# A decode block with a cached attention: wo behind the last values in three parts, w2 without zero rows, and the first norm on columns

## The chip, the cores and the metric

The kernel runs on one NeuronCore of a Trainium2 chip. The core has TensorE (PE in the rows; PEld is its loading of weights), VectorE (DVE), ScalarE (ACT), GpSimd (POOL) and SyncE (SP), which here issues the loads, and 16 DMA engines that move them. The metric is the device time of one execution in microseconds; the times given are medians of several runs.

## The reference, cut to what matters

Two tokens (B = 2, one position each, D = 512) go through an attention over a cache (32 heads, 4096 keys each, head size 128) and a dense block with a mish activation (F = 1376). Both are modulated by a vector c.

```python
mod = (_silu(c) @ w_mod).reshape(c.shape[0], 6, 1, -1)
sa, ca, ga, sb, cb, gb = (mod[:, i] for i in range(6))
h = _layernorm(x) * (1 + ca) + sa
q = (h @ wq)                                # (2, 32, 1, 128) by heads
p = softmax(q @ k_cache^T * Dh ** -0.5)     # k_cache, v_cache: (2, 32, 4096, 128) fp32
x = x + ga * ((p @ v_cache) as rows @ wo)   # wo: (4096, 512)
h = _layernorm(x) * (1 + cb) + sb
t = h @ w1 + b1                             # w1: (512, 1376)
x = x + gb * ((t * tanh(softplus(t))) @ w2) # w2: (1376, 512)
```

The keys and values are 268 MB in fp32, and each is used once.

## The kernel before

SBUF holds three "rooms" of 64 KB a partition, and everything large passes through them. A list `plan` fixes the order of the loads, and each entry names the room it fills and what must have been used before (`holds`); `used(...)` marks something as used and issues, on SP's queue, every load at the head of the list that may go. In order: `first` (w_mod's first five parts with b1), wq, the keys of head 0, then for heads 1 to 31 a "pair" of 8192 KB (the keys of head h and the values of an earlier one, `behind(h)`; heads 8 and 16 come alone with 4096 KB), then `load_wo` (wo's rows of 30 heads), `load_two` (values of heads 29 and 30, two transfers), `load_last` (values of head 31 in two transfers, wo's last two heads, w1 in two halves) and `load_tail` (mod5 and w2, four transfers; the first holds mod5 and five chunks of w2).

At the start, c and x come by a small transfer of their own (`cx`). x's first norm works on rows: `centred` and `rstd` on a 128x128 layout, with a matmul for the mean (L210) and one for the variance (L216), and the modulation of ca and sa is applied to rows and turned to columns once (L288).

In the loop over heads VectorE multiplies the keys by the query (`products`, L336) and sums them (`scores`, L340). The softmax is short work on VectorE, TensorE and ScalarE. TensorE multiplies values by the exponentials (`values`, L382). Heads are gathered in groups of four (`heads_out`: `totals`, `group_out`), the last four as two groups of two.

After the loop, `project` multiplies 30 heads by wo as rows into `att` (L422), which is copied to `att_sb` (L455) and turned into columns `xps` (L463); the mean of what is known by then (`near`, L481) is set aside. Then come the values of heads 30 and 31, and wo's last two heads are added to `xps` directly as columns (L491: 16 matmuls). From `xps` follow the second norm, w1 (`first_layer`), the activation (L572 to L580, into `actt`), mod5's modulation (L568), four matmuls that are a filler (`idle(4)`, L569), w2's matmuls (L585, chunk by chunk), two steps on VectorE and the output's transfer. w2 stands in 11 chunks of 128 rows, of which the last has 32 zero rows:

```python
WIDTHS = (384, 384, 352, 256)
CHUNKS = [(g, j) for j in range(3) for g in range(4) if WIDTHS[g] > P * j]
```

The program's order on each engine is the order in which it is written (`manual_schedule`), with waits put in for data.

Of the kernel before, what the change touches and what calls it, by code (L numbers as in the profile page):

```python
# [9 lines left out]
BF16 = mybir.dt.bfloat16  # L10
# [4 lines left out]
P = 128  # L15
# [15 lines left out]
WO_FIRST = H - 2  # L31
# [13 lines left out]
def kernel(ctx: ExitStack, tc: tile.TileContext, src: dict, out: bass.AP):  # L45
# [26 lines left out]
    cx = const.tile([16, P], F32, name="cx")  # L72
    nc.scalar.dma_start(out=cx, in_=src["cx"])

# [10 lines left out]
    b1_early = first[:, G * 5 * D :]  # L85
# [11 lines left out]
    def load_wo(n):  # L97
        late["wo"] = room(n, "wo")
        load(late["wo"], 0, src["wo"][:, : WO_FIRST * D])
        w_t["wo"] = late["wo"].rearrange("p (h n) -> p h n", h=H)  # L100

    def load_two(n):
        t = room(n, "two")
        for i in range(2):
            v_t[H - 3 + i] = heads(load(t, i * KV, src["single"][3 + i]))

    def load_last(n):
        t = room(n, "last")
        whole = src["single"][5]
        for a, z in ((0, 6), (6, 8)):  # L110
            load(t, a * KV // 8, whole[:, a * KV // 8 : z * KV // 8])
        v_t[H - 1] = heads(t[:, :KV])
        lo = KV
        load(late["wo"], WO_FIRST * D, src["wo"][:, WO_FIRST * D :])
        w_t["w1"] = t[:, lo : lo + G * F].rearrange("p (k n) -> p k n", k=G)
        for half in (src["w1"][:, : G * F // 2], src["w1"][:, G * F // 2 :]):
            load(t, lo, half)
            lo += G * F // 2
# [33 lines left out]
    def used(*items):  # L152
# [17 lines left out]
    mean_w = const.tile([P, G, R], F32, name="mean_w")  # L170
    nc.vector.tensor_scalar(
        out=mean_w, in0=fold[:, None, :].to_broadcast([P, G, R]), scalar1=1.0 / D, scalar2=None, op0=ALU.mult
    )
    mean_w = mean_w.rearrange("p g r -> p (g r)")
# [29 lines left out]
    def centred(s):  # L204
        rs = const.tile([P, 8], F32, name="rs")
        xc = const.tile([P, P], F32, name="xc")
        sq = const.tile([P, P], F32, name="sq")
        nc.vector.tensor_reduce(out=rs[:, 0:1], in_=s, axis=AX.X, op=ALU.add)
        mps = small_ps("mean_a")
        nc.tensor.matmul(mps[:, 0:1], lhsT=mean_w, rhs=rs[:, 0:1], start=True, stop=True)  # L210
        nc.vector.tensor_scalar(out=xc, in0=s, scalar1=mps[:, 0:1], scalar2=None, op0=ALU.subtract)
        nc.vector.scalar_tensor_tensor(
            sq, xc, 1.0, xc, op0=ALU.mult, op1=ALU.mult, accum_out=rs[:, 1:2]
        )
        vps = small_ps("var_a")
# [3 lines left out]
    def rstd(var, rs):
        nc.scalar.activation(rs[:, 2:3], var, AF.Ln, bias=eps_t[:, 0:1])  # L220
        nc.vector.tensor_scalar(out=rs[:, 4:5], in0=var, scalar1=EPS, scalar2=None, op0=ALU.add)
        nc.scalar.activation(rs[:, 3:4], rs[:, 2:3], AF.Exp, scale=-0.5)
        nc.vector.scalar_tensor_tensor(
            rs[:, 5:6], rs[:, 3:4], rs[:, 4:5], rs[:, 3:4], op0=ALU.mult, op1=ALU.mult
        )
        nc.vector.tensor_scalar(
            out=rs[:, 5:6], in0=rs[:, 5:6], scalar1=-0.5, scalar2=1.5, op0=ALU.mult, op1=ALU.add
        )
        return rs[:, 3:4], rs[:, 5:6]
# [28 lines left out]
    def idle(n):  # L258
        for _ in range(n):
            nc.tensor.matmul(ov[1], lhsT=busy[:, 0:P], rhs=busy, start=True, stop=True)  # L260


    cps = small_ps("cps")[:, : 2 * G * B]
    nc.tensor.matmul(cps, lhsT=cx, rhs=ident[0:16, 0 : 2 * G * B], start=True, stop=True)
    cps, xtps = (cps[:, G * B * i : G * B * (i + 1)].rearrange("p (g b) -> p g b", b=B) for i in range(2))
    xps0 = small_ps("xps0")[:, :P]
    nc.tensor.matmul(xps0, lhsT=place.rearrange("p g r -> p (g r)"), rhs=cx, start=True, stop=True)
    sg = const.tile([P, G, B], F32, name="sg")
    nc.scalar.activation(sg, cps, AF.Exp, scale=-1.0)
    nc.vector.tensor_scalar(out=sg, in0=sg, scalar1=1.0, scalar2=None, op0=ALU.add)  # L270
    nc.vector.reciprocal(sg, sg)
    nc.vector.tensor_tensor(out=ct[:, :, 0:B], in0=cps, in1=sg, op=ALU.mult)
    nc.vector.tensor_copy(two(ct)[:, :, B - 1], ct[:, :, B - 1])
    xt = small("xt")
    nc.vector.tensor_copy(xt, xtps)
    xq = const.tile([P, P], F32, name="xq")
    nc.vector.tensor_copy(xq, xps0)

    xn = const.tile([P, P], F32, name="xn")
    xc, var, rs = centred(xq)  # L280
    y0, y1 = rstd(var, rs)
# [10 lines left out]
    sb, cb = keep(3, ps[:, 0, :]), keep(4, ps[:, 1, :])
    gat, cbt, scale_t = small("gat"), small("cbt"), small("scale_t")
    nc.vector.tensor_copy(gat, columns(ga, "gaps"))
    nc.vector.tensor_scalar(out=cbt, in0=columns(cb, "cbps"), scalar1=1.0, scalar2=None, op0=ALU.add)
    nc.vector.tensor_copy(h2t[:, :, 2 * B : 3 * B], columns(sb, "sbps"))
    nc.vector.tensor_copy(h2t[:, :, B : 2 * B], cbt)
    nc.vector.tensor_tensor(out=scale_t, in0=gat, in1=cbt, op=ALU.mult)
    b1 = const.tile([P, NJ * G * B], F32, name="b1")
    nc.gpsimd.tensor_copy(b1, b1_early)  # L300
# [73 lines left out]
    groups = [list(range(4 * i, 4 * i + 4)) for i in range(H // 4 - 1)] + [[H - 4, H - 3], [H - 2, H - 1]]  # L374
# [44 lines left out]
    def project(hs):  # L419
        for h in hs:  # L420
# [6 lines left out]
                stop=(h >= H - 2 - G),  # L427
# [33 lines left out]
    nc.tensor.matmul(fps, lhsT=ident, rhs=b1, start=True, stop=False, skip_group_check=True)  # L461
    for g in range(G):
        nc.tensor.matmul(  # L463
            xps[:, g], lhsT=late["att_sb"][:, P * g : P * (g + 1)], rhs=fold[:, 0:B],
            start=(g == 0), stop=False, skip_group_check=True,
        )

    def whole(t, name):
        ps = small_ps(name)[:, : G * B]
        nc.tensor.matmul(ps, lhsT=ones, rhs=t, start=True, stop=True)  # L470
        s = const.tile([P, B], F32, name=name)
        nc.vector.tensor_reduce(
            out=s, in_=over_g(ps.rearrange("p (g b) -> p g b", b=B)), axis=AX.X, op=ALU.add
        )
        return s

    xa, offset = small("xa"), small("offset")
    near = const.tile([P, B], F32, name="near")
    nc.vector.tensor_tensor(out=xa, in0=xps, in1=gat, op=ALU.mult)
    nc.vector.tensor_tensor(out=xa, in0=xa, in1=xt, op=ALU.add)  # L480
    near_sum = whole(xa, "near_sum")  # L481
# [179 lines left out]
```

## Time and profile before

| | |
|---|---|
| Median of 3 runs | 698.85 us (698.8 to 699.05) |
| The profiled execution | 698.93 us |
| its span, first to last instruction | 697.2 us |
| HBM read | 297.23 MB, 426 GB/s over the span |
| DVE busy | 587.6 us (84%) |
| PE busy | 292.9 us (42%) |
| mean granted TensorE clock | 0.66 of full speed |
| code loads (queue q8) | 13 packets, 0.21 MB |

The span is what the trace shows; 1.73 us of the profiled execution lie around it. Times in rows are microseconds from the span's start unless marked ns. "Issue to landing" of a transfer counts from its instruction on SP's queue to the semaphore.

### The profile page before, as it was taken

What the parts mean: (1) busy time and instruction counts of PE and PEld (TensorE: products, weight loads), DVE (VectorE), ACT (ScalarE), POOL (GpSimd) and SP (SyncE); (2) the same over time, 40 slices, a digit from 0 to 9 for tenths busy, and PEclk for the clock granted to TensorE, in tenths of its full rate; (3) what the DMA queues carried; (4) which work ended last, traced back from release to release, by engine and by line L of the source; (5) the groups of instructions that cost most, each with busy time, mean ns of one, the idle gap of its engine ahead of it and who ended that gap; (6) DMA issues with size and microseconds to landing.
All of it is one profiled execution on the core that took longest, in us unless ns stands there. A gap on an engine that the chain in (4) does not pass through costs nothing.

```text
span 697.2 us, 4054 instructions
## 1 busy us (share of the span) xinstructions
PE 292.9 (42%) x1679; PEld 100.6 (14%) x1680; DVE 587.6 (84%) x240; ACT 39.5 (6%) x187; POOL 4.7 (1%) x22
## 2 busy tenths in 40 slices
PE   2360435432350435443504453444322453443886
PEld 1110101110110101111101111111100111110244
DVE  3039999999899999999999999999999899999102
ACT  1000000000000000000000000000000000000000
POOL 2000000000000000000000000000000000000000
PEclk9775565666655666566655558665765566556879
DMA  9999999999999999999999999999999999999996
GB/s 407 406 448 425 432 456 429 422 429 440 445 429 425 426 440 440 432 430 416 446 440 430 432 432 437 432 429 440 429 433 432 426 440 432 433 432 413 434 418 252
DMA packets 6686, 297.49 MB, mean 427 GB/s; under 512 B 756, under 2 KB 780, under 8 KB 1292
## 3 DMA queue, kind: packets, MB, share of 16 engines
q1 hardware_dynamic: 6636, 297.23, 98.8%
q8 instruction: 13, 0.21, 0.1%
q14 instruction: 5, 0.04, 0.0%
q10 hardware_dynamic: 32, 0.01, 0.0%
HBM read 297.23 MB, written 0.00 MB: 426 GB/s over the span
## 4 chain that ended last, share of the span: by engine, by line
DMA 49%; DVE 45%; PE 5%; issue 0%; ACT 0%; SPq 0%; DVEq 0%
DMA kv<-in_pair 40%; DVE kv L336 22%; DVE s L340 21%; DMA two<-in_single 4%; PE ov L382 2%; DMA tail<-in_w 2%; DMA first<-in_mod 2%; PE modps L241 1%; DVE n L358 1%; DVE n L357 1%; PE yps L585 0%; PE otp L398 0%; PE att L422 0%; PE last_ps L463 0%; DVE m L350 0%
## 5 line engine op out<-in xcount | busy, mean ns | idle before, releaser
L336 DVE TENSOR_TENSOR kv<-kv,qb 128x8192 f32<-128x8192 f32 x32 | 277.9, 8684 | 44.2 <-DMA kv<-in_pair 22.5
L340 DVE TENSOR_REDUCE s<-kv 128x64 f32<-128x8192 f32 x32 | 277.4, 8667 | 0.0
L382 PE MATMUL ov<-kv,e 128*32 128x512 f32 x928 | 168.6, 893 | 5.2 <-ACT e L366 5.2
L362 PE MATMUL mb<-n,ones 2*128 2x2 f32 x64 | 17.7, 344 | 221.4 <-DVE n L358 221.4
L321 PE MATMUL qb<-q_sb,row_of 32*128 32x512 f32 x32 | 28.4, 1035 | 65.4 <-DVE kv L336 65.4
L382 PEld LDWEIGHTS ov<-kv,e 128*32 128x32 f32 x928 | 36.9, 156 | 118.7 <-issue 109.6
L362 PEld LDWEIGHTS mb<-n,ones 2*128 2x128 f32 x64 | 15.8, 303 | 230.3 <-issue 155.5
L352 PE MATMUL mt<-ident,m 128*2 128x128 f32 x64 | 13.7, 300 | 75.8 <-DVE m L350 75.8
L363 ACT COPY m<-mb 128x2 f32<-128x2 f32 x32 | 5.1, 160 | 532.2 <-PE mb L362 423.7
L366 ACT ACTIVATE e<-s,m 128x32 f32<-128x32 f32 x64 | 20.0, 314 | 1.2
L321 PEld LDWEIGHTS qb<-q_sb,row_of 32*128 32x128 f32 x32 | 8.8, 302 | 73.7 <-DVE kv L336 67.8
L352 PEld LDWEIGHTS mt<-ident,m 128*2 128x2 f32 x64 | 3.1, 82 | 97.4 <-DVE m L350 76.7
L410 DVE RECIPROCAL total<-l 128x8 f32<-128x8 f32 (+1 forms) x9 | 1.7, 184 | 14.7 <-PE l L408 14.7
L308 PE MATMUL qps<-wq,ht 128*32 128x512 f32 x64 | 9.5, 761 | 10.5 <-DMA wq<-in_wq 10.5
L366 ACT ACTIVATION_READ_ACCUMULATOR e<-s,m 128x1 f32 x64 | 11.9, 186 | 0.0
L398 PE MATMUL otp<-pick,o 128*128 128x8 f32 (+1 forms) x72 | 9.5, 258 | 3.9 <-ACT o L394 3.9
L382 PE MATMUL ov<-two,e 128*32 128x512 f32 x64 | 9.7, 763 | 0.3 <-DMA two<-in_single 0.3
L422 PE MATMUL att<-wo,ot 128*2 128x512 f32 x60 | 9.6, 742 | 0.4 <-DVE ot L401 0.3
L398 PEld LDWEIGHTS otp<-pick,o 128*128 128x128 f32 x72 | 8.7, 191 | 5.5 <-ACT o L394 5.5
L401 DVE TENSOR_TENSOR ot_last<-otp,total 128x4 f32<-128x4 f32 x1 | 0.2, 163 | 11.0 <-PE otp L398 11.0
L357 DVE TENSOR_REDUCE n<-mt 2x1 f32<-2x128 f32 x32 | 8.7, 272 | 0.5 <-PE mt L352 0.5
L394 ACT COPY o<-ov 128x512 f32<-128x512 f32 x9 | 5.3, 586 | 61.4 <-PE ov L382 61.4
(140 smaller groups left out, 107.2 us busy)
## 6 DMA issues: line engine op xcount, KB each, us to landing
kv<-in_single SPq DMA_DIRECT2D x3, 4096.0 KB, 31.1
two<-in_single SPq DMA_DIRECT2D x2, 4096.0 KB, 34.3
wo<-in_wo SPq DMA_DIRECT2D x1, 7680.0 KB, 39.1
first<-in_mod SPq DMA_DIRECT2D x1, 5132.0 KB, 15.1
last<-in_single SPq DMA_DIRECT2D x1, 3072.0 KB, 27.6
last<-in_w SPq DMA_DIRECT2D x2, 1376.0 KB, 34.7
tail<-in_w SPq DMA_DIRECT2D x1, 2304.0 KB, 16.2
last<-in_single SPq DMA_DIRECT2D x1, 1024.0 KB
```

The source lines that it names most:

```text
L241: nc.tensor.matmul(ps[R * g : R * (g + 1)], lhsT=ct[:, k, :], rhs=t[:, k, :].rearrange("p (m n) -> p m n", m=n)[:, :, P * g : P * (g + 1)] ...
L308: nc.tensor.matmul(ps[R * g : R * (g + 1)], lhsT=ht[:, k, :], rhs=w_t["wq"][:, k, 512 * c : 512 * (c + 1)], start=(k == 0), stop=(k == G - 1),
L321: nc.tensor.matmul(qb[:, b], lhsT=row_of[R * g : R * (g + 1), b], rhs=q_sb[R * g : R * (g + 1), half], start=True, stop=True,)
L336: nc.vector.tensor_tensor(out=k_t[h], in0=k_t[h], in1=qv, op=ALU.mult)
L340: nc.vector.tensor_reduce(out=s_t[h].rearrange("p b j -> p (b j)"), in_=k_t[h].rearrange("p b j d -> p (b j) d"), axis=AX.X, op=ALU.add,)
L352: nc.tensor.matmul(mps[h], lhsT=m_t[h][:, 0:2], rhs=ident, start=True, stop=True)
L357: nc.vector.tensor_reduce(out=n[:, 0:1], in_=mps[h], axis=AX.X, op=ALU.max, negate=True)
L362: nc.tensor.matmul(bps[:, 0:2], lhsT=ones[0:B, :], rhs=n[:, 1:3], start=True, stop=True)
L366: nc.scalar.activation(e_t[h % 4][b][:, :, lo : lo + 4], s_t[h][:, b].rearrange("p (c m) -> p c m", m=4), AF.Exp, bias=m[:, 2 + b : 3 + b] ...
L382: nc.tensor.matmul(ov[i % 2][R * g : R * (g + 1), :], lhsT=e_t[h % 4][b][:, c, :], rhs=v_t[h][:, b, 4 * c : 4 * c + 4, :].rearrange("p m d ...
L398: nc.tensor.matmul(tps[:, :n], lhsT=o[:, m, :], rhs=pick[:, m, at : at + n], start=(m == 0), stop=(m == 3))
L422: nc.tensor.matmul(att[R * g : R * g + B, :], lhsT=ot[:, B * h : B * (h + 1)], rhs=w_t["wo"][:, h, :], start=(h < G), stop=(h >= H - 2 - G),)
```

## The change

The first load carries c and x as columns beside b1, the transfer `cx` goes, and the first norm is computed on columns by functions that the second norm uses as well (`whole`, `centred`, `root`, `times_root`); ca and sa are turned to columns each. The mean `near` and `offset` are taken from x alone, at the start. The order of the late loads becomes: values of heads 29 and 30 in one transfer, values of head 31, all of wo in three parts (16, 12 and 4 heads), w1 in two halves, mod5 alone, w2 in five parts. All 32 heads are projected as rows after the last values; the direct addition of the last two heads as columns goes, and so do the two groups of two heads and the filler. w2's 12 chunks have 128 rows but for the last two, which have 64 and 32; these two come from sources of shape (8, 8, 512) and (4, 8, 512), cut from arrays with a ninth row of zeros that is not read, and their matmuls use only as many rows.

```diff
-WIDTHS = (384, 384, 352, 256)
+WIDTHS = (384, 384, 320, 288)
...
+SIZES = [min(P, WIDTHS[g] - P * j) for g, j in CHUNKS]
...
-WO_FIRST = H - 2
+WO_PARTS = (0, 16, 28, 32)
+PARTS = ((0, 6), (10, 11), (11, 12), (6, 9), (9, 10))
...
-    cx = const.tile([16, P], F32, name="cx")
-    nc.scalar.dma_start(out=cx, in_=src["cx"])
...
     def load_two(n):
-        t = room(n, "two")
-        for i in range(2):
-            v_t[H - 3 + i] = heads(load(t, i * KV, src["single"][3 + i]))
+        piece = load(room(n, "two"), 0, src["two"])
+        v_t[H - 3], v_t[H - 2] = heads(piece[:, :KV]), heads(piece[:, KV:])
...
+    def load_wo(n):
+        t = room(n, "wo")
+        w_t["wo"] = t.rearrange("p (h n) -> p h n", h=H)
+        for a, z in zip(WO_PARTS, WO_PARTS[1:]):
+            load(t, a * D, src["wo"][:, a * D : z * D])
+        for i in range(2):
+            load(late["w1"], i * G * F // 2, src["w1"][:, i * G * F // 2 : (i + 1) * G * F // 2])
...
     def load_tail(n):
         t = room(n, "tail")
...
+        w_t["mod5"] = load(t, 0, src["mod5"]).rearrange("p (k n) -> p k n", k=G)
+        w2 = t[:, G * D : (G + NCH) * D]
+        w_t["w2"] = w2.rearrange("p (c n) -> p c n", c=NCH)
+        for i, (a, z) in enumerate(PARTS):
+            nc.sync.dma_start(out=w2[: SIZES[a], a * D : z * D], in_=src["w2"][i])
...
-        (load_wo, None),
         (load_two, [("v", H - 3), ("v", H - 2)]),
         (load_last, None),
+        (load_wo, None),
...
+    def root(v_sum, name):
+        st = const.tile([P, 4, B], F32, name=f"st_{name}")
+        nc.scalar.activation(st[:, 0], v_sum, AF.Ln, bias=eps_t[:, 0:1], scale=1.0 / D)
+        nc.scalar.activation(st[:, 1], st[:, 0], AF.Exp, scale=-0.5)
...
+    early = const.tile([P, (NJ + 2) * G * B], F32, name="early")
+    nc.gpsimd.tensor_copy(early, early_in)
...
     ps = modulation("0", 0, 3, w_t["mod"])
...
+    mod = [keep("012", ps)]
     ps = modulation("3", 3, 2, w_t["mod"])
...
+    mod.append(keep("34", ps))
+
+    near = const.tile([P, B], F32, name="near")
+    near_sum = whole(xt, "x_sum_a")
+    h, sq = centred(xt, near_sum, "a")
...
+    times_root(root(whole(sq, "v_sum_a"), "a"), h)
+    nc.vector.scalar_tensor_tensor(h, columns(mod[0][:, 1], "caps"), 1.0, h, op0=ALU.add, op1=ALU.mult)
+    nc.vector.tensor_tensor(out=ht[:, :, 0:B], in0=columns(mod[0][:, 0], "saps"), in1=h, op=ALU.add)
...
-    groups = [list(range(4 * i, 4 * i + 4)) for i in range(H // 4 - 1)] + [[H - 4, H - 3], [H - 2, H - 1]]
+    groups = [list(range(4 * i, 4 * i + 4)) for i in range(H // 4)]
...
-    project(range(H - 4))
-    values(H - 3)
...
-    project((H - 4, H - 3))
...
+    for h in range(H - 3, H):
+        values(h)
+        heads_out(h)
...
+    project(range(H))
+    nc.scalar.copy(late["att_sb"], att)
     for g in range(G):
...
-    values(H - 2)
-    values(H - 1)
-    group_out(len(groups) - 1, ot_last)
-    for i in range(2):
-        for g in range(G):
-            nc.tensor.matmul(
-                xps[:, g],
-                lhsT=w_t["wo"][:, H - 2 + i, P * g : P * (g + 1)],
...
-    idle(4)
...
-    for n in range(NCH):
+    chunks = [n for a, z in PARTS for n in range(a, z)]
+    for n in chunks:
         for t in range(G):
             nc.tensor.matmul(
                 yps[R * t : R * (t + 1), :P],
-                lhsT=actt[:, n, :],
-                rhs=w_t["w2"][:, n, P * t : P * (t + 1)],
...
+                lhsT=actt[: SIZES[n], n, :],
+                rhs=w_t["w2"][: SIZES[n], n, P * t : P * (t + 1)],
...
+    def part(a, z):
+        size = SIZES[a]
+        if size == P:
+            return join(w2[:, a:z])
+        t = np.zeros((size // 8, 9, D), w2.dtype)
+        t[:, :8] = w2[:size, a].reshape(size // 8, 8, D)
+        return t
```

## Rows read from the trace of the kernel before

**Rows 1.** The page: DMA share in 40 slices (tenths), and VectorE's two costliest groups.
```profile
DMA  9999999999999999999999999999999999999996
...
L336 DVE TENSOR_TENSOR kv<-kv,qb 128x8192 f32<-128x8192 f32 x32 | 277.9, 8684 | 44.2 <-DMA kv<-in_pair 22.5
L340 DVE TENSOR_REDUCE s<-kv 128x64 f32<-128x8192 f32 x32 | 277.4, 8667 | 0.0
```

**Rows 2.** SP's queue in order of time, from 606 us: start, us, instruction, count.
```profile
606.88 0.33 SPq L69 DMA_DIRECT2D wo<-in_wo  x1
626.24 0.80 SPq L69 DMA_DIRECT2D two<-in_single  x2
645.59 0.80 SPq L69 DMA_DIRECT2D last<-in_single  x2
...
646.91 0.91 SPq L69 DMA_DIRECT2D last<-in_w  x2
672.92 1.75 SPq L69 DMA_DIRECT2D tail<-in_w  x4
```

**Rows 3.** The tail load's issues (first and last), and its last part's time to landing.
```profile
L69 SPq DMA_DIRECT2D tail<-in_w x4: 327/422/430, 672.9 to 674.2; - x4
...
tail<-in_w SPq DMA_DIRECT2D x1, 256.0 KB, 18.6
```

**Rows 4.** The chain that ended last, from 672 us: start, us, what.
```profile
672.92 16.16 DMA tail<-in_w
...
689.22 1.08 PE modps L241 x32
...
690.46 0.81 PE ov L260 x3
691.27 2.58 PE yps L585 x88
```

**Rows 5.** Windows of 1 us at the stream's end: busy time by engine, PEclk, DMA share, GB/s.
```profile
689.00:690.00 1.00, 0.78 (x29) 0.81 (x32) 0.64 (x4) 0.00 (x0) 0.00 (x0) 1.00 0.69 274
690.00:691.00 1.00, 0.84 (x15) 0.34 (x7) 0.00 (x0) 0.27 (x1) 0.00 (x0) 1.00 0.40 158
691.00:692.00 1.00, 1.00 (x32) 0.80 (x33) 0.00 (x0) 0.00 (x0) 0.00 (x0) 1.00 0.29 107
692.00:693.00 1.00, 1.00 (x48) 1.00 (x43) 0.00 (x0) 0.00 (x0) 0.00 (x0) 1.00 0.02 8
```

**Rows 6.** Windows of 4 us around the projection; the first busy time is TensorE's.
```profile
647.00:651.00 4.00, 3.80 (x22) 1.01 (x26) 0.37 (x1) 0.88 (x5) 0.00 (x0) 0.61 0.97 418
651.00:655.00 4.00, 4.00 (x40) 0.85 (x32) 0.00 (x0) 0.00 (x0) 0.00 (x0) 0.97 1.04 444
661.00:665.00 4.00, 3.75 (x15) 2.06 (x15) 0.34 (x2) 0.59 (x1) 0.00 (x0) 0.56 0.96 412
```

**Rows 7.** The timeline from 661 to 690 us: start, us, engine, line, instruction.
```profile
661.36 1.76 PE L422 MATMUL att<-wo,ot 128*2 128x512 f32 x4 [0.25 <-DVE ot L401]
...
663.20 0.59 ACT L455 COPY last<-att 128x512 f32<-128x512 f32 x1 [3.20 <-DMA two<-in_single]
...
678.88 1.95 PE L491 MATMUL last_ps<-ot_last,wo 128*128 128x2 f32 x16 [0.25 <-DVE ot_last L401]
680.86 0.17 DVE L502 TENSOR_TENSOR u<-last_ps,scale_t 128x8 f32<-128x8 f32 x1 [2.04 <-PE last_ps L491]
...
689.58 0.20 DVE L580 TENSOR_TENSOR last<-f 128x22 f32<-128x22 f32 x1
```

**Rows 8.** The timeline of the start, to 36 us.
```profile
7.49 0.18 ACT L269 ACTIVATE sg<-cps 128x8 f32<-128x8 f32 x1 [5.04 <-PE cps L264]
...
8.44 0.17 DVE L273 COPY ct<-ct 128x4 f32<-128x4 f32 x1
...
23.72 0.33 SPq L69 DMA_DIRECT2D kv<-in_pair  x1
...
35.30 1.08 PE L308 MATMUL qps<-wq,ht 128*32 128x512 f32 x4 [10.53 <-DMA wq<-in_wq]
```

More of the change, by code (lines that the diff above doesn't have):

```diff
@@ L95, in load_keys @@
         k_t[h], v_t[behind(h)] = heads(piece[:, :KV]), heads(piece[:, KV:])
[L97 to L100, printed above, removed]
     def load_two(n):
-        t = room(n, "two")
-        for i in range(2):
-            v_t[H - 3 + i] = heads(load(t, i * KV, src["single"][3 + i]))
+        piece = load(room(n, "two"), 0, src["two"])
+        v_t[H - 3], v_t[H - 2] = heads(piece[:, :KV]), heads(piece[:, KV:])
     def load_last(n):
         t = room(n, "last")
[L109 to L118, printed above, removed]
+        v_t[H - 1] = heads(load(t, 0, src["single"][3]))
+        late["w1"] = t[:, KV : KV + G * F]
+        w_t["w1"] = late["w1"].rearrange("p (k n) -> p k n", k=G)
+        lo = KV + G * F
         for name, n_cols in (("att_sb", 512), ("hq_pad", NJ * P), ("actt", NCH * R)):
@@ L219, in rstd, with whole @@
[L219 to L224, printed above, removed]
-        )
[L226 to L229, printed above, removed]
+    def whole(t, name):
+        ps = small_ps(name)[:, : G * B]
+        nc.tensor.matmul(ps, lhsT=ones, rhs=t, start=True, stop=True)
+        s = const.tile([P, B], F32, name=name)
+        nc.vector.tensor_reduce(
+            out=s, in_=over_g(ps.rearrange("p (g b) -> p g b", b=B)), axis=AX.X, op=ALU.add
+        )
+        return s
@@ new lines, in centred @@
+    def centred(x, x_sum, name):
+        xm, sq = small(f"xm_{name}"), small(f"sq_{name}")
+        nc.vector.scalar_tensor_tensor(xm, each_g(x_sum), -1.0 / D, x, op0=ALU.mult, op1=ALU.add)
+        nc.vector.tensor_tensor(out=sq, in0=xm, in1=xm, op=ALU.mult)
+        return xm, sq
+    def root(v_sum, name):
+        st = const.tile([P, 4, B], F32, name=f"st_{name}")
+        nc.scalar.activation(st[:, 0], v_sum, AF.Ln, bias=eps_t[:, 0:1], scale=1.0 / D)
+        nc.scalar.activation(st[:, 1], st[:, 0], AF.Exp, scale=-0.5)
+        nc.vector.tensor_scalar(
+            out=st[:, 2], in0=v_sum, scalar1=-0.5 / D, scalar2=-0.5 * EPS, op0=ALU.mult, op1=ALU.add
+        )
+        return st
@@ L231, in columns, with times_root @@
+    def times_root(st, t):
+        for _ in range(2):
+            nc.vector.tensor_tensor(out=st[:, 2], in0=st[:, 2], in1=st[:, 1], op=ALU.mult)
+        nc.vector.tensor_tensor(out=t, in0=t, in1=each_g(st[:, 1]), op=ALU.mult)
+        nc.vector.scalar_tensor_tensor(t, each_g(st[:, 2]), 1.5, t, op0=ALU.add, op1=ALU.mult)
     def columns(s, name):
@@ L256, in small @@
         return const.tile([P, G, B], F32, name=name)
[L258 to L267, printed above, removed]
@@ L268 @@
-    sg = const.tile([P, G, B], F32, name="sg")
-    nc.scalar.activation(sg, cps, AF.Exp, scale=-1.0)
+    early = const.tile([P, (NJ + 2) * G * B], F32, name="early")
+    nc.gpsimd.tensor_copy(early, early_in)
+    c_in, xt = (early[:, G * B * i : G * B * (i + 1)].rearrange("p (g b) -> p g b", b=B) for i in range(2))
+    b1 = early[:, 2 * G * B :]
+    sg = small("sg")
+    nc.scalar.activation(sg, c_in, AF.Exp, scale=-1.0)
     nc.vector.tensor_scalar(out=sg, in0=sg, scalar1=1.0, scalar2=None, op0=ALU.add)
@@ L271 @@
     nc.vector.reciprocal(sg, sg)
-    nc.vector.tensor_tensor(out=ct[:, :, 0:B], in0=cps, in1=sg, op=ALU.mult)
+    nc.vector.tensor_tensor(out=ct[:, :, 0:B], in0=c_in, in1=sg, op=ALU.mult)
     nc.vector.tensor_copy(two(ct)[:, :, B - 1], ct[:, :, B - 1])
[L274 to L281, printed above, removed]
@@ L292 @@
[L292 to L296, printed above, removed]
+    ps = modulation("0", 0, 3, w_t["mod"])
+    mod = [keep("012", ps)]
+    ps = modulation("3", 3, 2, w_t["mod"])
+    mod.append(keep("34", ps))
@@ new lines @@
+    near = const.tile([P, B], F32, name="near")
+    near_sum = whole(xt, "x_sum_a")
+    h, sq = centred(xt, near_sum, "a")
+    nc.vector.tensor_scalar(out=near, in0=near_sum, scalar1=1.0 / D, scalar2=None, op0=ALU.mult)
+    times_root(root(whole(sq, "v_sum_a"), "a"), h)
+    nc.vector.scalar_tensor_tensor(h, columns(mod[0][:, 1], "caps"), 1.0, h, op0=ALU.add, op1=ALU.mult)
+    nc.vector.tensor_tensor(out=ht[:, :, 0:B], in0=columns(mod[0][:, 0], "saps"), in1=h, op=ALU.add)
+    gat, cbt, scale_t, offset = (small(n) for n in ("gat", "cbt", "scale_t", "offset"))
@@ L297 @@
+    nc.vector.tensor_copy(gat, columns(mod[0][:, 2], "gaps"))
+    nc.vector.tensor_scalar(
+        out=cbt, in0=columns(mod[1][:, 1], "cbps"), scalar1=1.0, scalar2=None, op0=ALU.add
+    )
+    nc.vector.tensor_copy(h2t[:, :, 2 * B : 3 * B], columns(mod[1][:, 0], "sbps"))
     nc.vector.tensor_copy(h2t[:, :, B : 2 * B], cbt)
     nc.vector.tensor_tensor(out=scale_t, in0=gat, in1=cbt, op=ALU.mult)
-    b1 = const.tile([P, NJ * G * B], F32, name="b1")
-    nc.gpsimd.tensor_copy(b1, b1_early)
+    nc.vector.tensor_tensor(out=offset, in0=xt, in1=each_g(near), op=ALU.subtract)
@@ L302 @@
+    nc.vector.tensor_tensor(out=offset, in0=offset, in1=cbt, op=ALU.mult)
     q_sb = const.tile([P, 2, 4 * DH], F32, name="q_sb")
@@ L464 @@
             xps[:, g], lhsT=late["att_sb"][:, P * g : P * (g + 1)], rhs=fold[:, 0:B],
[L465 removed]
+            start=(g == 0), stop=(g == G - 1), skip_group_check=True,
         )
[L468 to L481, printed above, removed]
[L482 to L501 removed]
+    u, x2, xg = small("u"), two(x2t), small("xg")
     nc.vector.tensor_tensor(out=u, in0=xps, in1=scale_t, op=ALU.mult)
     nc.vector.tensor_tensor(out=h2t[:, :, 0:B], in0=u, in1=offset, op=ALU.add)
[L504 to L510 removed]
+    nc.vector.tensor_tensor(out=xg, in0=xps, in1=gat, op=ALU.mult)
+    nc.vector.tensor_tensor(out=x2, in0=xg, in1=xt, op=ALU.add)
+    x_sum = whole(x2, "x_sum_b")
+    _, sq = centred(x2, x_sum, "b")
     w1ps = wide_ps("w1ps")
@@ L526 @@
     first_layer(0)
-    v_sum = whole(sq2, "v_sum")
+    v_sum = whole(sq, "v_sum_b")
     for k in range(1, G):
         first_layer(k)
-    st = const.tile([P, 6, B], F32, name="st")
-    nc.scalar.activation(st[:, 0], v_sum, AF.Ln, bias=eps_t[:, 0:1], scale=1.0 / D)
-    nc.scalar.activation(st[:, 1], st[:, 0], AF.Exp, scale=-0.5)
-    nc.vector.tensor_scalar(
-        out=st[:, 2], in0=v_sum, scalar1=-0.5 / D, scalar2=-0.5 * EPS, op0=ALU.mult, op1=ALU.add
-    )
+    st = root(v_sum, "b")
     nc.vector.scalar_tensor_tensor(st[:, 3], x_sum, 1.0 / D, near, op0=ALU.mult, op1=ALU.subtract)
@@ L586 @@
                 yps[R * t : R * (t + 1), :P],
[L587 to L590 removed]
+                lhsT=actt[: SIZES[n], n, :],
+                rhs=w_t["w2"][: SIZES[n], n, P * t : P * (t + 1)],
+                start=(n == chunks[0]),
+                stop=(n == chunks[-1]),
             )
@@ L634, in _lay_out @@
         "wo": join(rows(a["A_wo"])),
-        "w2_0": join(wm[:, :, 5 * D :], w2[:, :5]),
         "w1": join(rows(a["B_w1"])),
-        "w2_1": join(w2[:, 5:8]),
-        "w2_2": join(w2[:, 8:10]),
-        "w2_3": join(w2[:, 10:]),
+        "two": join(head_rows(v, H - 3), head_rows(v, H - 2)),
+        "mod5": join(wm[:, :, 5 * D :]),
+        **{f"w2_{i}": part(*p) for i, p in enumerate(PARTS)},
     }
@@ L654 @@
         ).ap()
-    src["w2"] = [src.pop(f"w2_{i}") for i in range(4)]
+    src["w2"] = [src.pop(f"w2_{i}") for i in range(len(PARTS))]
+    src["w2"] = [t[:, :8] if len(t.shape) == 3 else t for t in src["w2"]]
     out = nc.dram_tensor("out", inputs["A_x"].shape, F32, kind="ExternalOutput").ap()
```

81 lines of the change are left out of this document (8 added, 73 removed).

## Prediction

> **What bounds the kernel now.** I read the page's slices first. The DMA engines are at nine tenths or more in 39 of 40 slices, while VectorE spends 8.68 + 8.67 = 17.35 us on a head [rows 1]. Then SP's queue: it issues 8192 KB on a room's release every 19.35 us (606.88, 626.24, 645.59), so a load takes longer than VectorE's two passes, and two loads are always in flight [rows 2]. Hence the stream of bytes sets the time, at 8192 / 19.35 = 423 KB/us; a chunk of w2 (128 rows, 256 KB over sixteen engines) is worth 0.605 us. Only two things can move the end: how many bytes the busiest DMA engine carries, and what follows the last landing.
>
> Next the landings. The last part of w2 is issued at 674.2 and lands 18.6 later, at 692.8 [rows 3]. The chain shows that the end does not hang on it: it goes through the first part of the tail load (mod5 and five chunks in one transfer, landed at 689.09), then modps 1.08, the filler of `idle` 0.81, and the matmuls of w2, 2.58, up to 693.85 [rows 4]. From there to the span's end at 697.2 are 3.35 us, which both kernels pay. So about one microsecond lies between the last landing and the end of w2's matmuls, and most of it is modps and filler waiting behind a large first part.
>
> Last, how the stream ends. The DMA share falls to 0.69, 0.40 and 0.29 in the three microseconds from 689, and to 0.02 from 692 [rows 5]. A quarter of the engines, some four of sixteen, still work more than a microsecond after the rest are done. If all ended together, it would be near 689 + 0.69 + 0.40 + 0.29 + 0.02 = 690.4, two microseconds earlier. No view says which engines these are.
>
> **Part by part.** *First norm on columns.* c and x now ride at the end of the first load, so SiLU starts at its landing, not before it: from the exponential to ct took 7.49 to 8.61, 1.1 us, plus the small copy on POOL [rows 8]. Modulation starts about 1.5 us later and releases its room at some 25.2 instead of 23.72. The norm's two sums now stand behind both modulations on TensorE, so ht comes near 29. Both are covered: SP has 8192 KB of wq and 4096 KB of keys queued in front, and wq's matmuls wait for their load until 35.30 after 10.53 us of idleness [rows 8]. Cost nothing; without that cover 1.5 us. The cx transfer (8 KB) goes and its bytes come back in the first load: nothing.
>
> *Order of the loads.* The bytes are the same, and SP's rooms are released by the same scores as before (606.88, 626.24, 645.59), so the stream has no new hole. The tail load waits for the values of heads 29 and 30. Their room now lands near 648, so it is issued before 662 instead of 672.92, while the queue holds work until 684. SP issues 5 transfers after 645.59 in place of 5, and 6 in place of 4 in the tail, 0.43 each, all into a full queue: nothing.
>
> *w2's parts.* Before, every engine carried eleven chunks. The last 96 rows now come from sources whose leading sizes are 8 and 4. I take it that they go to eight and to four engines: then eight engines carry ten chunks, four carry eleven and four twelve. If the late engines are among the eight, the last landing moves from 692.8 to 692.2. Spread evenly (10.75 chunks) it is 692.65; if the late ones carry twelve it is 693.4. I take 692.2: eight of sixteen engines win, four lose, and the end is set by engines that were late already. The Trainium skill ("DMA: Bandwidth & Descriptors", Rules for kernel authors) says to use all 16 engines, since a leading dimension below 16 confines a transfer to that many; by it the four doubly loaded engines would end the stream at 693.4. The ends in [rows 5] are uneven, which that rule does not weigh, and they do not say which engines are late. The same page (Why a DMA increments its semaphore by 16 and not by 1) has the count as the largest number up to 16 that divides both leading sizes, and the engines as the lowest numbered; no row here shows it.
>
> *Landings counted back from 692.2* at 423 KB/us, on an engine with ten chunks: last chunk 692.2; three before it 691.6; the first six 689.8; mod5 (1024 KB) 686.15; w1's halves 683.7 and 680.5; wo's parts (4096, 3072, 1024 KB) 667.5, 674.8 and 677.2; the last values 657.9.
>
> *The projection.* All heads now go as rows, behind the landings. Values of head 31 (32 matmuls, at 3.8 us for 22 in the slower stretch) and the group's output are done before 667.5. Such a matmul took 4.00/40 = 0.10 us at clock 0.97 and 3.80/22 = 0.17 at 0.61 [rows 6]. The first 16 heads (32 matmuls) take 3.2 to 5.5 us and are done by 673. The next 12 (24) start at 674.8 and take 2.4 to 4.1; the last 4 (8) start at 677.2 and take 0.8 and 0.5 of drain. I take the faster pace, since TensorE has worked from 667.5 on: 678.6. Copy to att_sb 0.59 plus 0.1 [rows 7]: 679.3. Eight column matmuls are half of sixteen that took 1.95 [rows 7]: 680.3. Before, u started at 680.86 [rows 7]. So the chain that follows is some 0.5 us early.
>
> *From u to the activation.* Nothing in it changes but a few columns in a copy. It took 680.86 to 689.78 [rows 7], 8.92: now 680.3 to 689.2. mod5 has long landed, so modps (1.08) runs right behind the hidden layer's matmuls, from some 687.6, under the vector work; filler 0.81 is gone.
>
> *w2's matmuls.* They wait for the first six chunks: 689.8 and 0.05. Twelve chunks at 2.58/11 each are 2.81: 692.7. The last chunk landing at 692.2 allows 692.2 + 0.05 + 0.23 and a drain of 0.25, 692.75. So 692.75 against 693.85: **1.1 us less**. The profiled execution took 698.93 with 1.73 us around its span, and the median is 0.08 below it: 698.85 - 1.1 = 697.75, which I round up to **697.9** for the 64 and 128 KB transfers and their unseen price.
>
> *Removed and costed at nothing:* the row form's small constants and copies on VectorE before 16 us, one group output and the near_sum step in the tail; they lay beside loads or in the chain already replaced. Bounds: nothing to 0.3 us gained.
>
> **What the clock may do.** The stretches in [rows 6] show both levels, 0.5 and 1.0 of full speed (1.2 and 2.4 GHz), as means: 0.61 while TensorE came out of light work, 0.97 once it had run dense matmuls. At 661 to 665 it was back at 0.56, after some two microseconds of small matmuls [rows 6], and the two heads projected there took 1.76 [rows 7]. The Trainium skill ("TensorE: Matmul & The Clock Gate", HAM oscillation) says that waits for loads between bursts gate TensorE to 1.2 GHz each time. By that rule the new projection, which waits for three landings, would run at half clock: the second rival. The row at 651 is against it for dense work, the one at 661 for it behind a lull.
>
> **Rivals.** (1) *The late engines are not among the eight.* For: [rows 5] don't name them, and half of all engines lie elsewhere. Against: only four of sixteen lose. Spread evenly or on engines that keep eleven chunks: first six chunks 0.45 to 0.6 later, end at 693.2 to 693.3, 698.3. On the four with twelve: 693.4 + 0.53 = 693.9, 698.9.
>
> (2) *TensorE falls to half clock in the projection's waits; this is the slower side.* Place: between the first and second part of wo it idles one to three microseconds. Price: 32 matmuls at twice 0.10 from 674.8 are 6.4, then 0.5 of drain, copy 0.7, columns 1.9: 684.3 instead of 680.3; activation 693.2, w2's matmuls 696.0, against 693.85: 2.15 more, 701.0. If the clock comes back half way, 2 us of it are lost: about 699.0. It decides from the point where u starts later than 682.1 (even), and by 0.2% later than 683.5. Against: the burst before the wait is dense and the wait short. Without the filler the same fall could strike w2's matmuls themselves: 5.6 from 689.85 is 695.5, 700.5.
>
> (3) *The lateness goes away.* If the four engines are late by chance of this arrangement (code loads, order of transfers), the stream ends by 691.5 and only the activation at 689.2 binds: 692.1, 697.1.
>
> (4) *Nothing happens*, as the end hangs on the stream: gains of landing and tail cancel against later chunks. That is rival 1 in numbers, 698.3 to 698.9.
>
> **How the numbers follow.** Forecast 0.50, 697.9, own range 697.1 to 698.6. Rival 1 with 4: 0.22 (698.3 to 698.9). Rival 2: 0.16, of which 0.10 beyond 700.2. Rival 3: 0.12, 697.1. What a measurement here can tell from no change is about 0.2%, 1.4 us: below 697.45 is faster, above 700.25 slower. Faster: 0.12 and a fifth of the forecast's half, 0.22. Slower: 0.10. Same: 0.68. The range 697.1 to 699.4 leaves out the deep end of rival 3 and the slow part of rival 2.
>
> **What would show it.** Right: chain through the last parts of the tail load, with modps ahead of the activation; the tail load issued before 662; w2's matmuls starting near 689.9 and ending near 692.8 with waits for chunks; projection's last matmuls near 678.5 at clock 1.0. Wrong: u after 682, or a DMA share that keeps a quarter after 692; w2's matmuls well over 0.03 us apiece; modulation or wq's matmuls late enough that a load's issue moves from 606.88.

## The result and the profile after

The kernel after took 700.85 us (median of 20 runs, 699.58 to 702.07), the one before 699.0 (20 runs, 698.48 to 700.55): ratio 1.0022, 95% interval 1.0015 to 1.0029 (ratios here are taken over all runs; the two medians alone give 1.0026). That is slower, by a little over the 0.2% named in the prediction; forecast were 697.9 and a range of 697.1 to 699.4. The profiled execution of after took 701.02 us, with a span of 699.2.

The chain that ended last in after, from 656 us (start, us, what), which answers to [rows 4]:

```profile
656.27 0.33 SPq L70
656.60 0.44 issue
657.04 33.72 DMA tail<-in_w
690.76 0.14 issue
690.90 5.09 PE yps L514 x96
695.99 0.03 issue
```

Two numbers hold the loss. The first part of w2, its first six chunks, lands at 690.76 (657.04 + 33.72) where the forecast had 689.8. And the 96 matmuls of w2 take 5.09 us where it had 2.81. They end at 695.99, against 693.85 before.

Windows of 1 us of after (start:end, us, busy time of PE, PEld, DVE, ACT and POOL, PEclk, DMA share, GB/s), to be held against [rows 5]:

```profile
686.00:687.00 1.00, 0.82 (x10) 0.80 (x14) 0.00 (x0) 0.48 (x4) 0.00 (x0) 1.00 1.01 281
687.00:688.00 1.00, 1.00 (x33) 0.75 (x32) 0.59 (x4) 0.23 (x1) 0.00 (x0) 1.00 0.99 289
688.00:689.00 1.00, 0.02 (x4) 0.00 (x0) 0.55 (x3) 0.27 (x1) 0.00 (x0) 1.00 0.94 231
689.00:690.00 1.00, 0.00 (x0) 0.00 (x0) 0.00 (x0) 0.00 (x0) 0.00 (x0) 1.00 1.00 297
690.00:691.00 1.00, 0.10 (x4) 0.13 (x8) 0.00 (x0) 0.00 (x0) 0.00 (x0) 1.00 0.80 279
691.00:692.00 1.00, 1.00 (x37) 1.00 (x40) 0.00 (x0) 0.00 (x0) 0.00 (x0) 0.88 0.47 190
692.00:693.00 1.00, 1.00 (x23) 0.62 (x19) 0.00 (x0) 0.00 (x0) 0.00 (x0) 0.50 0.28 100
```

The same view of before, for the microsecond ahead of [rows 5]:

```profile
688.00:689.00 1.00, 0.15 (x2) 0.06 (x1) 0.49 (x3) 0.22 (x1) 0.00 (x0) 1.00 0.95 381
```

Read the last two columns together. From 686 to 690 the DMA engines of after are busy (0.94 to 1.01), and yet move only 231 to 297 GB/s; from 685 to 686 it was 406, and before had 381 from 688 to 689 at a share of 0.95. So the engines do not wait for work: each transfer takes longer. The packets in the trace (the pieces that a transfer is cut into, with the time of each) say the same: those of the first six chunks, 12288 bytes each, took 460 to 472 ns from 684 to 685 and 615 to 791 ns from 686 to 690, without exception. Then read PEclk: TensorE does nothing from 688.0 to 690.9, keeps its full clock to nearly 692, and then runs at 0.50 (1.2 GHz), in the middle of w2's matmuls.

The timeline of after (start, us, engine, line, instruction, idle time before it), beside [rows 7]:

```profile
667.00 5.71 PE L399 MATMUL att<-wo,ot 128*2 128x512 f32 x32 [4.09 <-DMA wo<-in_wo]
...
674.22 3.62 PE L399 MATMUL att<-wo,ot 128*2 128x512 f32 x32 [1.50 <-DMA wo<-in_wo]
...
679.63 0.17 DVE L444 TENSOR_TENSOR u<-last_ps,scale_t 128x8 f32<-128x8 f32 x1 [16.75 <-PE last_ps L436]
...
686.94 1.08 PE L227 MATMUL modps<-tail,ct 128*32 128x128 f32 x32
...
688.45 0.20 DVE L508 TENSOR_TENSOR last<-f 128x24 f32<-128x24 f32 x1
690.87 1.60 PEld L514 LDWEIGHTS yps<-tail,last 128*32 128x32 f32 x48 [3.11 <-issue]
690.90 5.05 PE L514 MATMUL yps<-tail,last 128*32 128x128 f32 x96 [2.88 <-DMA tail<-in_w]
```

Up to the activation the forecast holds. wo's parts land at 666.9 and 674.2 (forecast 667.5 and 674.8); the projection is done at 677.84 (forecast 678.1 without its drain), u starts at 679.63 (680.3), modps at 686.94 (687.6), and the activation ends at 688.65 (689.2). All is 0.3 to 0.7 us early, and then TensorE waits 2.88 us for a landing.

### The profile page after: what moved, and what is told of

Same layout as the page of the kernel before. It is cut to its first block, busy times and chain, and to the rows that moved or that the text cites. A ratio compares the mean times of both kernels' runs of the same rounds, so it can differ in the third digit from the quotient of the medians.

```text
span 699.2 us, 3990 instructions
## 1 busy us (share of the span) xinstructions
PE 281.3 (40%) x1658; PEld 94.4 (14%) x1658; DVE 582.5 (83%) x230; ACT 39.4 (6%) x185; POOL 4.5 (1%) x21
## 4 chain that ended last, share of the span: by engine, by line
DMA 52%; DVE 42%; PE 4%; issue 0%; SPq 0%; POOL 0%; ACT 0%; DVEq 0%
DMA kv<-in_pair 45%; DVE kv L313 21%; DVE s L317 20%; DMA tail<-in_w 5%; DMA first<-in_mod 2%; PE ov L359 2%; PE modps L227 1%; PE yps L514 1%; DVE n L335 1%; PE qb L298 1%; DVE n L334 0%; DVE m L327 0%; PE mb L339 0%; SPq L70 0%; PE mt L329 0%
## 5 line engine op out<-in xcount | busy, mean ns | idle before, releaser
L359 PE MATMUL ov<-kv,e 128*32 128x512 f32 x928 | 162.7, 866 | 5.0 <-ACT e L343 5.0
L227 PE MATMUL modps<-first,ct 128*32 128x384 f32 (+1 forms) x64 | 7.0, 609 | 17.7 <-DVE ct L254 17.7
L387 DVE RECIPROCAL total<-l 128x8 f32<-128x8 f32 x8 | 1.5, 187 | 13.6 <-PE l L385 13.6
L375 PE MATMUL otp<-pick,o 128*128 128x8 f32 x64 | 8.5, 259 | 3.2 <-ACT o L371 3.2
```

The lines of the kernel that those rows point to most:

```text
L227: nc.tensor.matmul(ps[R * g : R * (g + 1)], lhsT=ct[:, k, :], rhs=t[:, k, :].rearrange("p (m n) -> p m n", m=n)[:, :, P * g : P * (g + 1)] ...
L359: nc.tensor.matmul(ov[i % 2][R * g : R * (g + 1), :], lhsT=e_t[h % 4][b][:, c, :], rhs=v_t[h][:, b, 4 * c : 4 * c + 4, :].rearrange("p m d ...
L375: nc.tensor.matmul(tps[:, :n], lhsT=o[:, m, :], rhs=pick[:, m, at : at + n], start=(m == 0), stop=(m == 3))
```

## Experiments

Two causes were to be told apart: the clock (a filler gone, a wait of 2.88 us) and the landings (something in the new parts of w2 slows every transfer). A third question was whether the forecast's choice of engines was right.

**1. after with a filler** behind mod5's modulation: twelve matmuls on a tile of zeros, `idle` as in before.

```diff
...
     gps = modulation("5", 0, 1, w_t["mod5"])
+    idle(12)
```

> The changed kernel with twelve filler matmuls between mod5's modulation and w2's matmuls, so that TensorE is busy until the first six chunks of w2 land. Theory A (two costs: the stream's last microseconds are slowed, and TensorE, idle for 2.9 us before w2's matmuls, falls to half clock in them): the 96 matmuls run at 0.03 us apiece, about 2.8 us in place of 5.1, first six chunks still land near 690.8; end of w2's matmuls near 693.8, time near 699.0, ratio to before 0.999 to 1.001. Theory B (the late landings alone cost the time): the end moves by less than 0.5 us, ratio 1.0015 to 1.003. Theory C (the filler is all that was lost): the ratio falls below 0.9985, since the shorter path pays out.

Measured: 699.68 us (11 runs), 1.0012 [1.0003, 1.0021], span 697.5. From its chain, then its window at 692:

```profile
657.04 33.84 DMA tail<-in_w
690.88 0.14 issue
691.01 3.27 PE yps L521 x96
```

```profile
692.00:693.00 1.00, 1.00 (x36) 0.57 (x27) 0.00 (x0) 0.00 (x0) 0.00 (x0) 1.00 0.31 107
```

The landing is as late as in after (690.88), the clock stays at 1.00, and the 96 matmuls take 3.27 us instead of 5.09. So the clock is a cause, worth 1.82 us in these profiles and 0.0010 of the ratio (some 0.7 us; the two intervals overlap, after's runs lie 2.5 us apart, and its profiled execution is above their median). What remains, 1.0012, is not of the clock; it is a little more than I had thought would remain.

**2. after with plain w2:** eleven chunks of 128 rows again, the zero rows back; the rest of the change stays.

```diff
-WIDTHS = (384, 384, 320, 288)
+WIDTHS = (384, 384, 352, 256)
-SIZES = [min(P, WIDTHS[g] - P * j) for g, j in CHUNKS]
+SIZES = [P] * NCH
-PARTS = ((0, 6), (10, 11), (11, 12), (6, 9), (9, 10))
+PARTS = ((0, 6), (6, 9), (9, 10), (10, 11))
```

> The changed kernel with w2 as before: eleven chunks of 128 rows, the last with 32 zero rows, in four parts, every part over all rows. Theory A: the DMA engines keep above 380 GB/s until 689, the first six chunks land near 690.0 and the last near 692.8; TensorE still idles some 2 us before w2's matmuls, so the clock can still fall in some executions: ratio 0.9990 to 1.0015, with a spread of over 1 us. Theory B: the ratio is 0.999 or less in all executions. Theory C: as the changed kernel, 1.0015 to 1.003.

Measured: 698.36 us, 0.9991 [0.9982, 1.0], span 696.5. Its windows:

```profile
686.00:687.00 1.00, 0.94 (x14) 0.93 (x18) 0.07 (x1) 0.38 (x4) 0.00 (x0) 1.00 1.01 424
687.00:688.00 1.00, 0.90 (x32) 0.63 (x24) 0.64 (x5) 0.26 (x2) 0.00 (x0) 1.00 1.00 410
688.00:689.00 1.00, 0.00 (x0) 0.00 (x0) 0.42 (x3) 0.23 (x1) 0.00 (x0) 1.00 0.91 363
```

With 64 KB more to move, the stretch that ran at 231 to 289 GB/s runs at 363 to 424, and w2's matmuls start before 690. The 96 thin rows are worth 0.0031 of the ratio (1.0022 less 0.9991), the filler's 0.0010 among them: without the late landing the wait is 1.69 us, and in this execution the clock stays up by itself. The edit also drops the twelfth chunk and changes the order of the parts; number 7 keeps both as in after. The rest of the change gains 0.0009, some 0.6 us, with an interval that touches 1.

**3. after with plain w2 and a filler:** the edit of 2 with `idle(8)`.

> The changed kernel with w2 as before (128-row chunks) and eight filler matmuls, 1.7 us, between mod5's modulation and w2's matmuls. Theory A: the stream ends as with plain w2 (0.9991), the clock can no longer fall in the wait: ratio 0.9980 to 0.9992, and a narrower spread. If the last landing alone sets the end: the same ratio as with plain w2, to 0.0003.

Measured: 698.36 us, 0.9986 [0.9978, 0.9995]: the one version here whose interval lies wholly below 1. From 2 it can't be told.

**4. after, thin parts over sixteen engines:** the sources are (64, 512) and (32, 512), without the ninth row.

```diff
-        t = np.zeros((size // 8, 9, D), w2.dtype)
-        t[:, :8] = w2[:size, a].reshape(size // 8, 8, D)
-        return t
+        return np.ascontiguousarray(w2[:size, a])
```

> The changed kernel with the parts of 64 and 32 rows from sources without the ninth row, shapes (64, 512) and (32, 512), so that they can spread over all sixteen engines. If confinement to eight and four engines slows the stream (theory A): the stretch of 231 to 297 GB/s from 687 to 690 is gone, as with plain w2, and the first six chunks land before 690.2. If thin parts as such slow it: the stretch stays under 300 GB/s and the landing is 690.5 or later. The clock's share of the cost is the same in both: ratio 1.000 to 1.002.

Measured: 701.38 us (6 runs), 1.0031 [1.0019, 1.0043]. From 688 to 691 it moved 227, 281 and 213 GB/s at shares of 0.94, 0.91 and 0.86, and the first six chunks landed at 690.97 (656.99 + 33.98). The trace also has the steps in which a transfer's semaphore rises as its shares land: sixteen for each full part, eight and four for the thin parts of after, sixteen for each thin part here. So the thin parts did go over more engines, and that cures nothing: the number of engines is not the cause.

**5. before without its filler:** `idle(4)` goes.

> The kernel before without its four filler matmuls. Theory A: TensorE waits only 1.1 us there and modps directly precedes w2's matmuls, so the clock holds; 0.8 us come off the path: ratio 0.9985 to 0.9995. Theory C (the filler is what held the clock): w2's matmuls take over 4 us in place of 2.6, ratio 1.0005 to 1.002.

Measured: 698.71 us, 0.9995 [0.9986, 1.0005]. TensorE waited 0.77 us in front of w2's 88 matmuls, the clock kept 1.00 from 689 to 694, and they took 2.64 us. So in this execution the filler was not needed. Its 0.8 us had been on the path, but the ratio does not tell its removal from nothing.

**6. after, the 96 rows as three parts of 32,** from sources of shape (8, 4, 512) cut out of (8, 5, 512): eight engines, each with four neighbouring rows.

```diff
...
+            for r in range(0, SIZES[a] % P, R):
+                nc.sync.dma_start(out=w2[r : r + R, a * D : z * D], in_=src["w2"][i][r // R])
...
-        t = np.zeros((size // 8, 9, D), w2.dtype)
-        t[:, :8] = w2[:size, a].reshape(size // 8, 8, D)
+        t = np.zeros((size // 32, 8, 5, D), w2.dtype)
+        t[:, :, :4] = w2[:size, a].reshape(size // 32, 8, 4, D)
...
```

> The changed kernel with w2's last 96 rows in three parts of 32 rows from sources of shape (8, 4, 512), so eight engines take four neighbouring rows each. Theory D (a part over fewer than 128 rows makes engines write into rows that others are writing, and slows all of them; four neighbouring rows to an engine avoid it): 1-us windows from 686 to 689 stay above 380 GB/s, w2's matmuls start before 690.2, and, if the late engines are not among these eight, the last landing is near 692.1 and the ratio 0.9975 to 0.9990. Theory E (any part of few rows, or small sources, slow the stream): 231 to 310 GB/s from 687 to 690 as in the changed kernel, ratio 1.001 to 1.003. If the late engines are among the eight: no slow stretch, last landing 693.2 or later.

Measured: 698.47 us, 0.9992 [0.9983, 1.0]. Its windows, and the end of its chain:

```profile
686.00:687.00 1.00, 1.00 (x18) 0.98 (x22) 0.18 (x1) 0.21 (x2) 0.00 (x0) 1.00 1.03 422
687.00:688.00 1.00, 0.76 (x28) 0.49 (x20) 0.67 (x4) 0.39 (x2) 0.00 (x0) 1.00 0.94 383
688.00:689.00 1.00, 0.00 (x0) 0.00 (x0) 0.29 (x2) 0.10 (x1) 0.00 (x0) 1.00 0.96 387
...
691.00:692.00 1.00, 1.00 (x32) 0.60 (x32) 0.00 (x0) 0.00 (x0) 0.00 (x0) 1.00 0.14 39
692.00:693.00 1.00, 0.77 (x29) 0.50 (x20) 0.09 (x1) 0.00 (x0) 0.00 (x0) 1.00 0.00 0
```

```profile
658.27 31.13 DMA tail<-in_w
689.40 0.14 issue
689.54 3.28 PE yps L517 x96
692.81 0.03 issue
```

The same bytes on as few rows, and the slow stretch is gone (383 to 422 GB/s from 686 to 689). So neither thin transfers nor small ones are the cause as such; what is left is which engine writes which rows. In this execution the forecast's choice of engines holds too: the DMA share from 691 to 692 is 0.14 against 0.29 before, and nothing moves after 692. The semaphores say it directly. Each of the eight shares of the first thin part lands 0.3 us behind a share of the first six chunks, the last at 688.24; the four latest shares of the six chunks land from 689.11 to 689.40. So none of the four late engines is among the eight with thin rows.

**7. after, the thin parts landing wide:** the same 128 and 64 KB on 128 rows, 256 and 128 columns wide.

> The changed kernel with the same 96 rows' bytes (128 and 64 KB sources, same place in the order) landing over all 128 rows, 256 and 128 columns wide; the last two chunks' products then multiply the wrong numbers, the work is the same. Theory D (where the bytes land is what slows): no stretch under 350 GB/s before 689, first six chunks land before 690.2. Theory E (small sources or small transfers slow): 231 to 310 GB/s from 687 to 690, first six chunks at 690.6 or later.

Measured: 698.22 us, 0.9989 [0.9979, 1.0]. Its windows:

```profile
686.00:687.00 1.00, 1.00 (x12) 0.23 (x5) 0.00 (x0) 0.16 (x1) 0.00 (x0) 0.54 1.04 415
687.00:688.00 1.00, 0.80 (x8) 0.71 (x6) 0.00 (x0) 0.59 (x4) 0.00 (x0) 1.00 1.01 390
688.00:689.00 1.00, 1.00 (x34) 0.85 (x33) 0.51 (x3) 0.22 (x1) 0.00 (x0) 1.00 0.90 357
```

Size, place in the queue and w2's twelve chunks are as in after. What differs is the rows on which the parts land and, with them, the length of the piece for a row (1024 and 512 bytes in place of 2048), and the cost is gone.

**8. after, one part of 96 rows** from a (96, 512) source, eleven chunks.

> The changed kernel with eleven chunks as before, the last of them one part of 96 rows without zero rows, shape (96, 512), on sixteen engines with six rows each. Theory D: the engines write into each other's rows, a slow stretch of under 320 GB/s somewhere from 686 to 690, though shorter than with two thin parts; ratio 1.0005 to 1.0025. If only parts on few engines or of 64 and 32 rows slow the stream: as with plain w2, ratio 0.998 to 0.9995.

Measured: 699.92 us, 1.0011 [1.0003, 1.002]; 268, 346, 262 and 293 GB/s from 686 to 690, first six chunks at 690.72. A single part with 96 rows slows the rest too. The clock fell here as well. The wait in front of w2's matmuls, then the clock around it:

```profile
690.87 4.20 PE L514 MATMUL yps<-tail,last 128*32 128x128 f32 x88 [1.65 <-DMA tail<-in_w]
```

```profile
690.00:691.00 1.00, 0.14 (x4) 0.17 (x8) 0.00 (x0) 0.00 (x0) 0.00 (x0) 0.89 0.70 242
691.00:692.00 1.00, 1.00 (x24) 1.00 (x26) 0.00 (x0) 0.00 (x0) 0.00 (x0) 0.50 0.39 156
```

The wait is 1.65 us, shorter than the 1.69 of number 2 and the 1.77 of number 6, which left the clock at 1.00. So the length of the wait alone does not say whether the clock falls.

**9 and 10. The version of 6 with `idle(8)`, and with its first part split in two.**

```diff
-PARTS = ((0, 6), (10, 11), (11, 12), (6, 9), (9, 10))
+PARTS = ((0, 3), (3, 6), (10, 11), (11, 12), (6, 9), (9, 10))
```

> The kernel with w2's last 96 rows in three parts of 32 rows and eight filler matmuls between mod5's modulation and w2's matmuls. If the clock falls in the wait in some executions with three parts alone (its runs go from 698.0 to 700.2), the filler takes the high ones away: nearly all runs under 699.0, ratio 0.9980 to 0.9990. If those high runs have another cause, they stay, and the ratio is 0.9988 to 0.9996.

> The kernel with w2's last 96 rows in three parts of 32 rows, and its first six chunks in two parts of three, so that w2's matmuls can begin when the activation is ready. Theory F (with the slow stretch gone, what is left is TensorE's wait for the first six chunks and its 3.3 us after it): w2's matmuls start near 688.5, end near 692.5, ratio 0.9975 to 0.9990 and below that of the three parts alone (0.9992). If the last landing alone sets the end: ratio as with the three parts, to 0.0003, since it does not move.

Measured: 698.57 us, 0.9988 [0.9976, 1.0], and 698.71 us, 0.9992 [0.9978, 1.0006]. Neither can be told from 6. Five of the filler's twelve runs still lie at 699.4 to 699.7, so why some runs are a microsecond longer stays open. With the split, w2's matmuls start at 689.05, but a part lands at 692.30, and TensorE stands idle for 1.07 us before it. The semaphores show what was different in this execution: one share of each thin part landed behind all of the first six chunks (689.83 for 689.52), so one of the late engines was among the eight with thin rows, and the last landing came at 692.9 in place of 691.9 in 6.

**11. before with its last chunk on 96 rows** (a (96, 512) source in place of 128 rows with zeros).

```diff
...
-        "w2_3": join(w2[:, 10:]),
+        "w2_3": np.ascontiguousarray(w2[:96, 10]),
```

> The kernel before, with only its last part of w2 changed: 96 rows, shape (96, 512), in place of 128 rows with 32 of zeros. Theory D (rows of a part that covers fewer than 128 collide with what other engines write): the last microseconds of the stream are slower although 64 KB are gone, the last landing is 0.3 to 1.0 us later, ratio 1.0003 to 1.0015. If fewer bytes simply end earlier: ratio 0.9995 to 1.0000.

Measured: 699.06 us, 0.9996 [0.9985, 1.0008]. The windows of this run:

```profile
688.00:689.00 1.00, 0.65 (x8) 0.59 (x6) 0.00 (x0) 0.73 (x4) 0.00 (x0) 1.00 0.95 330
689.00:690.00 1.00, 1.00 (x35) 0.96 (x34) 0.39 (x3) 0.22 (x1) 0.00 (x0) 1.00 0.72 217
```

They moved 330 and 217 GB/s where before moved 381 (its line is in the section on the result) and 274 [rows 5], at nearly the same shares: the slow stretch is there in the kernel before as well, though shorter. I had expected the time to follow; it did not. The chain there goes through modps, the filler and w2's matmuls (691.22 to 693.81), as in [rows 4], and the last landing stays at 692.9 with 64 KB less to move. The 88 matmuls took 2.59 us, as before's 2.58.

## Why the prediction was wrong

**The step that failed: "w2's parts".** It costed the two thin parts by the bytes that each engine carries, and put 0.15 us on their "unseen price". In fact they slow all transfers that are in flight beside them, to some 230 to 300 GB/s over five microseconds: the first six chunks land at 690.76 for 689.8, the last part at 693.4 (676.7 + 16.7) for 692.2. Engines without such rows are slowed as well: the four that land last, none of them among the eight of the 64-row part, took 5.0 us from the landing of their shares of mod5 to that of their shares of the six chunks, and 3.7 in 6. Experiments 4, 6, 7 and 8 narrow what it hangs on: not the number of engines (4), not the size of the parts or their place in the queue (7), not 32 rows as such (6). What is left is the pattern in which engines write rows. Why that slows everything, no run here can show. The Trainium skill ("DMA: Bandwidth & Descriptors", The descriptor swizzle) describes a transfer to 128 rows as one in which each engine writes one port of SBUF, in blocks of four neighbouring rows. Number 6 has one such block for each engine in a transfer, and is fast; in number 4, by the page's count, blocks of rows that share a port (0 to 3 and 32 to 35) would come from two engines if they are dealt out in order. Both agree with a reading by ports, but no run here shows a port, and why engines without thin rows are slowed stays open, so it remains a reading.

**The step that this set off: the clock.** The prediction named it, in the last sentence of rival 2: "Without the filler the same fall could strike w2's matmuls themselves", priced at 5.6 us and 700.5. It took 5.09, and 700.85. But it stood there as an aside to the projection, and the path's landing was put at 689.8. With that landing the wait would have been about one microsecond. Whether the clock would then have stayed up is not shown for certain: it did in 2 and 6, where TensorE idles 1.69 and 1.77 us before w2's matmuls, and it did not in 8, where it idles 1.65. In these profiles the clock fell only where a late landing and a removed filler came together: 1 has the first alone, 2 the second alone, and in both it is 1.00; 4 and 8 have both, and it is 0.50. In the projection the clock did fall, and it cost little: 20 matmuls ran at 0.50 from 667 to 671, while wo's second part was still on its way, and the 32 behind that landing ran at 1.00 (3.62 us).

**A term that was mis-sized.** Twelve chunks at full clock take 3.23 to 3.28 us (1 and 6), not 2.81. Timeline of number 6, pauses in brackets:

```profile
690.98 0.15 PEld L517 LDWEIGHTS yps<-tail,last 64*32 64x32 f32 x8 [0.20 <-issue]
691.34 0.15 PEld L517 LDWEIGHTS yps<-tail,last 32*32 32x32 f32 x8 [0.20 <-issue]
691.68 0.81 PEld L517 LDWEIGHTS yps<-tail,last 128*32 128x32 f32 x32 [0.20 <-issue]
```

At each of these changes of the number of rows (128 to 64, 64 to 32, 32 to 128) the loading of weights pauses for 0.20 us, and the excess is 0.42 to 0.47. It is not so for every change: number 11 goes from 128 to 96 rows for its last chunk without a pause.

**What adds up.** Start of w2's matmuls 1.05 late (690.90 for 689.85), clock 1.82 (5.09 less 3.27), pauses 0.46 (3.27 less 2.81): 3.33, against a miss of 3.24 at the end of w2's matmuls (695.99 for 692.75; the forecast had 0.09 there for the last chunk's landing).

**What was right.** The thin parts did go to eight and to four engines (number 4 has the counts). The norm on columns cost nothing: SP issued at 606.88 and 626.24 as before [rows 2]. The stream kept no hole, and the tail load was issued at 656.27, before 662. Projection, u, modps and activation came 0.3 to 0.7 us before their forecast. The choice between the ends of the stream, that the late engines are among the eight with ten chunks, holds in the profile of 6 and fails for one engine in that of 10: it changes from one profile to the next, and nothing in [rows 5] could tell it. Where it held, it was luck. It also gains nothing over 2 (0.9992 and 0.9991): with the last landing at 691.9, the 3.28 us of matmuls behind 689.54 set the end, 692.81.

## What to carry to other kernels

Cost a load by the rows on which it lands and the engines that write them, not by its bytes alone: 192 KB on 64 and 32 rows, which saved 64 KB, took about a third of the rate from all that flew beside them (289 GB/s for 410 from 687 to 688). When a filler is taken out, ask how long TensorE would then wait if the landing behind it were a microsecond late, and what half clock would cost: a wait of 2.88 us in front of the last matmuls was followed by half clock, which cost 1.82, and of three waits of about 1.7 one was. And chunks of 64 and 32 rows between full ones are not free on TensorE either.

## What was not expected of the hardware

The busy share of the DMA engines stays at one while their rate falls to 231 GB/s: share alone does not show a slow transfer, the last column does. And SP stands for long in the tail's issues. Its queue and its waits in after (waited for: us in total, times, longest):

```profile
657.04 19.97 SPq L123 DMA_DIRECT2D tail<-in_w  x5
```

```profile
SPq L123 <- DMA wo<-in_wo: 17.2, 3, 8.4
```

Five issues took 19.97 us, where before's four took 1.75 [rows 2], and 17.2 of them were waits that ended with the landing of wo's parts. No data ties w2 to wo; the semaphores do. In the trace the loads on SP's queue raise eight semaphores in turn, and a load is issued only when the one eight places ahead of it has landed: the 32-row part, eight places behind wo's first part, was issued at 666.89, right behind that part's landing at 666.87. In before, the loads eight places ahead had landed when w2's were issued. Number 6 has the same (18.6 us in four waits), and is fast: it did no harm, since the queue held work throughout.
